# Plain blocks of a fused attention and two-layer MLP kernel: the second product two steps behind the first, s r + b in a buffer of its own, low halves of x on VectorE, attention's mean later

## The chip, the cores and the metric

The kernel runs on one core of a Trainium2 chip. A core has five engines that run side by side and meet at semaphores: TensorE (PE in the rows; its weight loads stand as PEld), VectorE (DVE), ScalarE (ACT), GpSimd (POOL) and SyncE (SP), whose queue issues every DMA here. Matrix products land in eight PSUM banks of 128 x 512 fp32 numbers, everything else is in SBUF or in DRAM. The metric is device time in microseconds (us), median of several runs.

## What is computed

Attention without softmax, normed by row, then two MLPs, all in fp32:

```python
kv = np.einsum('bhsd,bhse->bhde', k, v)          # 8 batches, 8 heads, 576 tokens, 64 wide
out = np.einsum('bhsd,bhde->bhse', q, kv)
out = out / np.sqrt(np.mean(out * out, axis=-1, keepdims=True) + 1e-06) * g_norm
x = out.transpose(0, 2, 1, 3).reshape(4608, 512)
r = np.maximum(x @ w_in, 0.0)                    # first MLP, 512 -> 2048 -> 512
x = (s * (r * r) + b) @ w_out
h = x @ w2_in                                    # second MLP, same sizes
y = (h * (1.0 / (1.0 + np.exp(-1.702 * h)))) @ w2_out
```

The weights arrive as 64-bit numbers and are brought to fp32 on ScalarE and VectorE.

## The kernel before

**Tiling.** The 4608 tokens are nine blocks of 512; features lie on the partitions, so a block of x is four tiles of 128 x 512. To keep fp32 accuracy at TensorE's faster format, each operand is split into a high part (rounded) and a low part (the rest): `xh`, `xl` of x, `gh`, `gl` of the activation, and two halves of each weight tile `w`. A product is then three matmuls: high by high, high by low, low by high.

**Stages.** The first MLP does blocks 0, 1, 2 plainly (`plain`) and the other six in pairs, with the first product by Strassen's seven products (`first_products`) and the second plainly (`second_plain`). The second MLP does four pairs with Strassen in both products and its last block plainly. Attention for block j is computed some time before block j is needed, in four units p (`attention`): `att_product` (o_ps), `att_square` (sq and, from block 2 on, its high part sh), `att_low` (sl), `att_mean` (ms, a product with a matrix of averages), `att_root` (three ScalarE steps), `att_newton` (three VectorE steps, after which the banks of o_ps and ms are free) and `att_split` (xh and xl, or a store to DRAM for blocks from 3 on). The K'V products of the later batches (`kv_product`, a tile kvs each) run between the steps of blocks 0 and 1.

**A plain block.** Sixteen steps f. `mlp_h` makes the first product of a step (twelve matmuls into a bank h), `mlp_act` relu and square into r, `mlp_g` the operand s r + b: gh from r on ScalarE (L447), then on VectorE r itself becomes s r + b in place (L448), then gl = r - gh (L451). `mlp_o` makes the second product of the step (twelve matmuls into four banks o that are summed over all steps); in the order of the program it stands one step behind the first product.

**Weights.** In block 0 both weights of each step are made from raw words: `w_low` (two ScalarE instructions, ca and cu), `w_words` (L144, L145, L150, L151 on VectorE), `w_hi` (L161, ScalarE) and `w_lo` (L166, VectorE). There are thirty such weights after the first two.

**What sets the order.** A table. Each piece of work is entered with a slot, a number (`at`); at the end the entries are sorted and written out, and each engine takes its own instructions in that order. A step of a plain block is two slots: the first product at 2f, activation and second product of the step before at 2f + 1. `kv_work` enters K'V loads and products, `attend` the units of attention with a list of seven gaps (product, square, low, mean, root, Newton, split) from the unit's first slot. `Slots` hands out PSUM banks and SBUF tiles, the one free longest first.

Of the kernel before, what the change touches and what calls it, by code (L numbers as in the profile page):

```python
# [7 lines left out]
F32 = mybir.dt.float32  # L8
# [3 lines left out]
ALU = mybir.AluOpType  # L12
# [5 lines left out]
NP = H // 2  # L18
NF = DFF // P
# [17 lines left out]
NBIG, NMID = 42, 22  # L37
NPLAIN = 3
LEAD = 4
G1_ACT = (0, 0, 0, 1.5, 0.2, 1.6, 1.6)  # L40
OPS = ("A11", "S2", "S3", "S1", "A12", "A22", "S4", "A21")
PRODUCTS = (("A11", "B11"), ("S2", "T2"), ("S3", "T3"), ("S1", "T1"), ("A12", "B21"), ("A22", "T4"), ("S4", "B22"))
# [18 lines left out]
def kernel(ctx: ExitStack, tc: tile.TileContext, qT, kv_h, kvt, cst,  # L61
# [7 lines left out]
    pe, act, dve, pool = nc.tensor, nc.scalar, nc.vector, nc.gpsimd  # L69
# [9 lines left out]
    def new(slots, shape, dtype, name):  # L79
        t, n = slots.take(shape, dtype, name)  # L80
        where[id(t)] = (slots, n, t)
        return t

    def drop(*tiles):
        for t in tiles:
            slots, n, _ = where.pop(id(t))
            slots.give(n)

    def new4(dtype, name):
        return new(big, [P, 2, T], dtype, name)  # L90

    def new2(dtype, name):
        return new(mid, [P, T], dtype, name)
# [8 lines left out]
    s_col, b_col = cst_sb[:, 1:2], cst_sb[:, 2:3]  # L102
# [267 lines left out]
    def att_split(j, p):  # L370
        x = att.pop((j, p))
        if j >= NPLAIN:
            nc.sync.dma_start(out=xd[0][j][p], in_=x)
            drop(x)
            done.add((0, j, p))
            return
        if p == 0:
            xT[0, j] = []
        if p % 2 == 0:
            xT[0, j].append((new4(F32R, "xh"), new4(F32R, "xl")))  # L380
        xh, xl = xT[0, j][p // 2]
        if j:
            act.activation(xh[:, p % 2, :], x, AF.Copy)
        else:
            dve.tensor_copy(out=xh[:, p % 2, :], in_=x)  # L385
        pool.tensor_sub(out=xl[:, p % 2, :], in0=x, in1=xh[:, p % 2, :].bitcast(F32))  # L386
        drop(x)
        done.add((0, j, p))

# [53 lines left out]
    def mlp_g(m, j, f):  # L443
        r = G[m, j, f]
        gh, gl = G[m, j, f] = new2(F32R, "gh"), new2(F32R, "gl")
        if m == 0:
            act.activation(gh, r, AF.Identity, scale=s_col, bias=b_col)  # L447
            dve.tensor_scalar(out=r, in0=r, scalar1=s_col, scalar2=b_col, op0=ALU.mult, op1=ALU.add)  # L448
        else:
            act.activation(gh, r, AF.Copy)  # L450
        dve.tensor_sub(out=gl, in0=r, in1=gh.bitcast(F32))  # L451
        drop(r)
# [218 lines left out]
    def at(slot, fn, *a):  # L671
        events.append((slot, len(events), fn, a))

    def weight(load, slot, gap, conv_at, *unit):
        at(load, w_load, *unit)
        for i, fn in zip(conv_at, (w_low, w_words, w_hi, w_lo)):
            at(slot + gap * i, fn, *unit)

    def kv_work(load, slot, b, p):
        at(load, kv_load, b, p)  # L680
        at(slot, kv_product, b, p)
        if b:
            at(slot + 2, kv_store, b, p)

    def attention(slots, j, p):
        for slot, fn in zip(slots, (att_product, att_square, att_low, att_mean, att_root, att_newton, att_split)):
            at(slot, fn, j, p)

    def plain(m, j, base, last):
        base -= 0.005  # L690
        for f in range(NF):
            at(base + 2 * f, mlp_h, m, j, f)
            at(base + 2 * f + 1, mlp_act, m, j, f)
            if f:
                at(base + 2 * f + 1, mlp_o, m, j, f - 1)
                if last:
                    at(base + 2 * f + 1, wo_done, m, f - 1)
            at(base + 2 * f + 1.01, mlp_g, m, j, f)
        end = base + 2 * NF + 1
        at(end - 0.01, mlp_o, m, j, NF - 1)  # L700
        if last:
            at(end - 0.01, wo_done, m, NF - 1)
        at(end + 0.02, mlp_store, m, j)

    def first_products(m, base, shift):
        for i in range(NF // 2):
            for k in range(len(PRODUCTS)):
                slot = base + 3.5 * i + 0.5 * k + (shift if i or k > 1 else 0)
                at(slot, g1_product, m, i, k)
                at(slot + 0.52, g1_sum, m, i, k)  # L710
                at(slot + 0.72 + G1_ACT[k], g1_act, m, i, k)
                if k % 2 == 0:
                    at(slot - LEAD, op_load, m, i, k // 2)
            if i % 2 and m == 0:
                for n, (q, fn) in enumerate((("22", AF.Relu), ("21", AF.Relu), ("22", AF.Square), ("21", AF.Square),
                                             ("12", AF.Relu), ("11", AF.Square), ("12", AF.Square))):
                    at(slot + 1.4 + 0.45 * n, r_act, q, i // 2, fn)
            elif i % 2:
                at(slot + 3.1, t_sums, i // 2)
        return base + 28 + shift  # L720

    def second_plain(j, base):
        for f in range(NF):
            at(base + 2 * f - LEAD, wo_load, 0, f)
            for n in range(2):
                slot = base + 2 * f + n
                at(slot, mlp_o, 0, j + n, f)
                if f % 4 < 2:
                    at(slot - 3.3, g2_scale, *quarter(f, n)[:2])
                at(slot - 2.5, g2_hi, 0, j + n, f, n)  # L730
                at(slot - 2.0, g2_lo, 0, j + n, f, n)
                if n:
                    at(slot, wo_done, 0, f)
        at(base + 31.1, mlp_store, 0, j)
        at(base + 32.1, mlp_store, 0, j + 1)
        return base + 32

    def second_products(j, base):
        for k in range(len(PRODUCTS)):
            for n in range(4):  # L740
                slot = base + 4 * k + n
                at(slot, g2_product, k, n)
                at(slot - LEAD, go_load, k, n)
                at(slot - 3.2, go_sum, k, n)
                at(slot - 2.4, go_hi, k, n)
                at(slot - 1.7, go_lo, k, n)
            for d in range(2):
                at(slot + 0.6 + 0.5 * d, g2_sum, j, k, d)
                if k > 2:
                    at(slot + 2.6, g2_store, j, k, d)  # L750
        return base + 28
# [55 lines left out]
    for p in range(NP):  # L807
        kv_work(-99 + p, START[p][0], 0, p)
        at(-99 + p, q_load, 0, p)
        o, m, n, x = START[p][1:]  # L810
# [2 lines left out]
    weight(-89, -48.5, 4, CONV[0], 0, 1, 0)  # L813


    for n, (f, w) in enumerate([(f - w, w) for f in range(1, NF + 1) for w in range(2) if f - w < NF][1:]):
        weight(n - 5, n - 1, 1, CONV[1], 0, f, w)


    for n in range(NP * (B - 1)):  # L820
        kv_work(2 * n - 8.9, 2 * n - 5, 1 + n // NP, n % NP)


    for j in range(NPLAIN):
        plain(0, j, 32 * j, j == NPLAIN - 1)
    base = 32 * NPLAIN
    firsts, seconds = {}, {}
    for j in range(NPLAIN, NB, 2):
        firsts[0, j] = base
        seconds[0, j] = first_products(0, base, j == NPLAIN)  # L830
        base = second_plain(j, seconds[0, j])
    for j in range(0, NB - 1, 2):
        firsts[1, j] = base
        seconds[1, j] = first_products(1, base, 0)
        base = second_products(j, seconds[1, j])
    plain(1, NB - 1, base, True)


    def attend(units, first, step, gaps):
        for u, (j, p) in enumerate(units):  # L840
            slot = first + step * u
            if p == 0 and j < B:
                at(slot - 2.2, kvbd_load, j)
            at(slot - 4, q_load, j, p)
            attention([slot + i for i in gaps], j, p)

    def units(*blocks):
        return [(j, p) for j in blocks for p in range(NP)]

    attend(units(1), 7, 6, (0, 0, 0, 2, 2, 4, 6))  # L850
    attend(units(2, 3), 34, 3.7, (0, 0.7, 1.3, 2, 2.5, 3.6, 6))
    attend(units(4), 65, 3, (0, 0.7, 1.3, 1.7, 2.2, 2.9, 4.5))
    for j in range(NPLAIN, NB - 2, 2):
        attend(units(j + 2, j + 3), firsts[0, j] + 0.4, 3.1, (0, 0.7, 1.3, 1.8, 2.3, 3.2, 5.5))


    x_operands(0, NPLAIN, 32 * NPLAIN - 14, 1.25)
# [11 lines left out]
    for k in range(2):  # L869
        slot = seconds[1, NB - 3] + 10 + 4 * k  # L870
# [10 lines left out]
    for i in range(NF // 2):  # L881
        slot = 50 + 5.4 * i
# [10 lines left out]
    slot = 32 * NPLAIN + 4  # L893
# [16 lines left out]

    for f in range(NF):
        at(base + 2 * f - LEAD, wi_load, 1, f)
        at(base + 2 * f + 2 - LEAD, wo_load, 1, f)

    events.sort(key=lambda e: e[:2])
    with tc.manual_schedule():
# [40 lines left out]
```

## Time and profile before

| | |
|---|---|
| median of 3 runs | 1606.41 us (1605.46 to 1606.84) |
| the profiled execution | 1604.21 us, of which the span from first to last instruction is 1602.4 us |
| TensorE busy | 1568.8 us, 98% of the span |
| VectorE busy | 1114.2 us, 70% |
| ScalarE busy | 846.3 us, 53% |
| GpSimd busy | 18.9 us, 1% |
| DMA | 385.36 MB, mean 240 GB/s |
| granted TensorE clock, mean | 0.996 of full |

The shares are means over stages that differ. Block 0 runs from about 28 to 167 us, block 1 to about 283, block 2 to about 383, then come the Strassen pairs, and the last plain block from about 1511 us on. In a row of the timeline the columns are start, duration, engine, line, operation, out<-in, shapes, count, and in brackets the engine's idle time just before and what ended it. Instructions of one engine overlap a little, so what one costs its engine is the distance to the next one's start.

### The profile page before, as it was taken

What the parts mean: (1) busy time and instruction counts of PE and PEld (TensorE: products, weight loads), DVE (VectorE), ACT (ScalarE), POOL (GpSimd) and SP (SyncE); (2) the same over time, 40 slices, a digit from 0 to 9 for tenths busy, and PEclk for the clock granted to TensorE, in tenths of its full rate; (3) what the DMA queues carried; (4) which work ended last, traced back from release to release, by engine and by line L of the source; (5) the groups of instructions that cost most, each with busy time, mean ns of one, the idle gap of its engine ahead of it and who ended that gap; (6) DMA issues with size and microseconds to landing.
All of it is one profiled execution on the core that took longest, in us unless ns stands there. A gap on an engine that the chain in (4) does not pass through costs nothing.

```text
span 1602.4 us, 19757 instructions
## 1 busy us (share of the span) xinstructions
PE 1568.8 (98%) x6932; PEld 1280.1 (80%) x6932; DVE 1114.2 (70%) x1621; ACT 846.3 (53%) x1261; POOL 18.9 (1%) x22
## 2 busy tenths in 40 slices
PE   7989999999999999999999999999999999999999
PEld 5766787778878887888888888888888888888887
DVE  6888346666888578784674378867986796688422
ACT  5767456655789468972694225512542353244222
POOL 1000000000000000000000000000000000000000
PEclk9999999999999999999999999999999999999999
DMA  7953646557978698976982585885688578736780
GB/s 239 308 183 103 207 150 206 205 195 246 326 282 294 220 383 286 323 252 262 342 307 80 203 302 200 285 301 212 238 270 302 187 276 274 270 120 220 240 293 27
DMA packets 172418, 385.36 MB, mean 240 GB/s; under 512 B 25120, under 2 KB 57888, under 8 KB 172320
## 3 DMA queue, kind: packets, MB, share of 16 engines
q1 hardware_dynamic: 172320, 384.11, 68.6%
q8 instruction: 55, 0.90, 0.2%
q14 instruction: 43, 0.35, 0.1%
HBM read 292.95 MB, written 91.10 MB: 240 GB/s over the span
## 4 chain that ended last, share of the span: by engine, by line
PE 60%; DVE 0%; issue 0%
PE o L632 19%; PE o L461 14%; PE d L504 7%; PE a L504 7%; PE b L504 3%; PE f L504 3%; PE c L504 3%; PE h L424 3%; DVE st L472 0%; DVE r L530 0%; DVE sl L342 0%; PE ms L350 0%; DVE op L229 0%
## 5 line engine op out<-in xcount | busy, mean ns | idle before, releaser
L461 PE MATMUL o<-gh,w 128*128 128x512 f32 x1280 | 407.5, 391 | 0.3
L461 PEld LDWEIGHTS o<-gh,w 128*128 128x128 f32 x1280 | 240.4, 188 | 51.8 <-ACT gh L447 2.0
L632 PE MATMUL o<-gh,wl 128*128 128x512 f32 x896 | 276.7, 389 | 0.0
L461 PE MATMUL o<-gl,w 128*128 128x512 f32 x640 | 251.0, 392 | 10.5 <-DVE gl L451 10.3
L632 PEld LDWEIGHTS o<-gh,wl 128*128 128x128 f32 x896 | 168.2, 188 | 34.9
L424 PE MATMUL h<-xh,w 128*128 128x512 f32 x512 | 176.7, 406 | 0.2 <-DVE xh L385 0.2
L632 PE MATMUL o<-gl,wl 128*128 128x512 f32 x448 | 174.5, 389 | 0.0
L504 PE MATMUL a<-xh,wl 128*128 128x512 f32 x448 | 157.5, 392 | 0.7 <-ACT c L520 0.7
L504 PE MATMUL d<-xh,wl 128*128 128x512 f32 x448 | 157.2, 392 | 0.3 <-DVE r L530 0.3
L461 PEld LDWEIGHTS o<-gl,w 128*128 128x128 f32 x640 | 120.2, 188 | 40.6 <-DVE gl L451 15.5
L424 PEld LDWEIGHTS h<-xh,w 128*128 128x128 f32 x512 | 97.3, 190 | 24.2 <-issue 1.0
L520 ACT ACTIVATE c<-a 128x512 f32<-128x512 f32 x56 | 33.3, 595 | 156.6 <-PE a L504 156.6
L424 PE MATMUL h<-xl,w 128*128 128x512 f32 x256 | 101.3, 396 | 1.9 <-POOL xl L386 1.9
L504 PEld LDWEIGHTS a<-xh,wl 128*128 128x128 f32 x448 | 84.1, 188 | 18.9 <-ACT c L520 1.1
L504 PEld LDWEIGHTS d<-xh,wl 128*128 128x128 f32 x448 | 84.1, 188 | 18.3 <-DVE r L530 0.8
L632 PEld LDWEIGHTS o<-gl,wl 128*128 128x128 f32 x448 | 84.1, 188 | 17.4
L575 DVE TENSOR_TENSOR gl<-r,gh 128x512 fp32r<-128x512 f32 x96 | 65.1, 688 | 38.8 <-ACT gh L570 36.8
L606 ACT ACTIVATE gh<-t 128x1024 fp32r<-128x1024 f32 x48 | 51.0, 1062 | 72.4 <-DVE t L597 62.3
L504 PE MATMUL a<-xl,wl 128*128 128x512 f32 x224 | 87.3, 390 | 0.0
L504 PE MATMUL d<-xl,wl 128*128 128x512 f32 x224 | 87.3, 390 | 0.0
L559 ACT ACTIVATE r<-r 128x1024 f32<-128x1024 f32 x84 | 84.8, 1047 | 0.0
L611 DVE TENSOR_TENSOR gl<-r,gh 128x1024 fp32r<-128x1024 f32 x64 | 77.2, 1219 | 7.2 <-ACT gh L606 7.2
(110 smaller groups left out, 2701.0 us busy)
## 6 DMA issues: line engine op xcount, KB each, us to landing
wl<-wsd SPq DMA_DIRECT2D x168, 512.0 KB, 7.0
wl<-wo2S SPq DMA_DIRECT2D x64, 512.0 KB, 5.7
wsd<-op SPq DMA_DIRECT2D x96, 256.0 KB, 3.8
w<-wod SPq DMA_DIRECT2D x48, 512.0 KB, 6.3
wl<-wo2A SPq DMA_DIRECT2D x48, 512.0 KB, 4.8
raw<-in_w_in SPq DMA_DIRECT2D x32, 512.0 KB, 7.1
kv_in<-in_kv SPq DMA_DIRECT2D x32, 512.0 KB, 4.9
raw<-in_w_out SPq DMA_DIRECT2D x32, 512.0 KB, 6.3
```

Source lines behind the costliest of these rows:

```text
L424: pe.matmul(h, lhsT=a, rhs=b, start=(n == 0), stop=(n == 3 * NP - 1))
L461: pe.matmul(acc[m, j][c], lhsT=a, rhs=x, start=(f == 0 and n == 0), stop=(f == NF - 1 and n == 2))
L504: pe.matmul(o, lhsT=a, rhs=b, start=(first and n == 0), stop=(n == 5), skip_group_check=not first)
L520: act.activation(st["c1"], st[0], AF.Copy)
L559: act.activation(R[q, n], R[q, n], fn)
L575: dve.tensor_sub(out=gl, in0=R[q, i][:, half, :], in1=gh.bitcast(F32))
L606: act.activation(hi, src, AF.Copy)
L611: dve.tensor_sub(out=lo, in0=src, in1=hi.bitcast(F32))
L632: pe.matmul(so[k, d], lhsT=a, rhs=b, start=(first and n == 0 and i == 0 and e == 0), stop=(n == 3 and i == 1 and e == 2), skip_group_check ...
```

## The change

`LAG = 2`: in a plain block the second product of step f stands at slot 2f + 4.99, two steps behind the first and not one; the store of the block's sums moves with it, and so do, by the same constant, the loads and the making of second weights, and the two places where the last plain block of the first MLP runs into the Strassen part (`first_products`' shift). `mlp_g` of the first MLP writes s r + b into a new tile g. The subtraction xl = x - xh goes from GpSimd to VectorE. K'V loads and products from the fourth on stand two slots later (product) and 2.4 slots later (load). Attention's units of block 1 start at 9.2, every 5 slots (before: 7, every 6), those of the first Strassen pair at 5.4 every 2.9 slots behind its start (before: 0.4 and 3.1), and the gaps change: mean, root and Newton step of blocks 2 to 4 stand about 0.5 to 0.8 slots later behind their product.

```diff
@@ att_split
-        pool.tensor_sub(out=xl[:, p % 2, :], in0=x, in1=xh[:, p % 2, :].bitcast(F32))
+        dve.tensor_sub(out=xl[:, p % 2, :], in0=x, in1=xh[:, p % 2, :].bitcast(F32))
@@ mlp_g
             act.activation(gh, r, AF.Identity, scale=s_col, bias=b_col)
-            dve.tensor_scalar(out=r, in0=r, scalar1=s_col, scalar2=b_col, op0=ALU.mult, op1=ALU.add)
+            g = new2(F32, "g")
+            dve.tensor_scalar(out=g, in0=r, scalar1=s_col, scalar2=b_col, op0=ALU.mult, op1=ALU.add)
+            drop(r)
+            r = g
@@ plain
-            if f:
-                at(base + 2 * f + 1, mlp_o, m, j, f - 1)
...
+            slot = base + 2 * f + 2 * LAG + 0.995
+            at(slot, mlp_o, m, j, f)
...
+        at(slot + 0.03, mlp_store, m, j)
@@ first_products
-                slot = base + 3.5 * i + 0.5 * k + (shift if i or k > 1 else 0)
+                slot = base + 3.5 * i + 0.5 * k + min(shift, (7 * i + k) // 2)
@@ weights, K'V and attention's slots
-    for n, (f, w) in enumerate([(f - w, w) for f in range(1, NF + 1) for w in range(2) if f - w < NF][1:]):
+    for n, (f, w) in enumerate([(f - LAG * w, w) for f in range(1, NF + LAG) for w in range(2) if 0 <= f - LAG * w < NF][1:]):
-        kv_work(2 * n - 8.9, 2 * n - 5, 1 + n // NP, n % NP)
+        kv_work(2 * n - (8.9 if n < 3 else 6.5), 2 * n - (5 if n < 3 else 3), 1 + n // NP, n % NP)
-    attend(units(1), 7, 6, (0, 0, 0, 2, 2, 4, 6))
-    attend(units(2, 3), 34, 3.7, (0, 0.7, 1.3, 2, 2.5, 3.6, 6))
-    attend(units(4), 65, 3, (0, 0.7, 1.3, 1.7, 2.2, 2.9, 4.5))
+    attend(units(1), 9.2, 5, (0, 0.2, 0.2, 1.8, 2, 3.6, 5.5))
+    attend(units(2, 3), 34, 3.7, (0, 0.7, 1.3, 2.6, 3.0, 4.0, 6))
+    attend(units(4), 65, 3.2, (0, 0.7, 1.3, 2.3, 2.7, 3.7, 5))
...
-        attend(units(j + 2, j + 3), firsts[0, j] + 0.4, 3.1, (0, 0.7, 1.3, 1.8, 2.3, 3.2, 5.5))
+        first, step = (5.4, 2.9) if j == NPLAIN else (0.4, 3.1)
+        attend(units(j + 2, j + 3), firsts[0, j] + first, step, (0, 0.7, 1.3, 1.8, 2.3, 3.2, 5.5))
@@ second weights of the last plain block
-        at(base + 2 * f + 2 - LEAD, wo_load, 1, f)
+        at(base + 2 * f + 2 * LAG - LEAD, wo_load, 1, f)
```

The order on ScalarE in block 0, in the step in which the first unit of block 1's attention takes its root (y), before (r is relu and square, w and ca, cu belong to weights):

```order
L436 ACTIVATE r<-h 128x512
L437 ACTIVATE r<-r 128x512
L161 ACTIVATE w<-ca 128x512
L297 ACTIVATE kvs<-kv 64x64
L357 ACTIVATE y<-ms,eps 128x512
L358 ACTIVATE y<-y 128x512
L359 ACTIVATE y_765<-y 128x512
L447 ACTIVATE gh<-r,cst_sb 128x512
L137 ACTIVATE ca<-raw 128x512
```

The same step after (lines are those of the changed file):

```order
L437 ACTIVATE r<-h 128x512
L438 ACTIVATE r<-r 128x512
L162 ACTIVATE w<-ca 128x512
L298 ACTIVATE kvs<-kv 64x64
L448 ACTIVATE gh<-r,cst_sb 128x512
L358 ACTIVATE y<-ms,eps 128x512
L359 ACTIVATE y<-y 128x512
L360 ACTIVATE y_826<-y 128x512
L138 ACTIVATE ca<-raw 128x512
```

The three steps of the root have moved from ahead of gh to behind it.

The order on VectorE in block 0, where that unit's Newton steps stand, before:

```order
L300 COPY kvs<-kv 64x64
L364 SCALAR_TENSOR_TENSOR y_765<-ms,y_765 128x512
L365 SCALAR_TENSOR_TENSOR y<-y_765,y 128x512
L366 SCALAR_TENSOR_TENSOR y_765<-o_ps,g_col,y 128x512
L448 TENSOR_SCALAR r<-r,cst_sb 128x512
L451 TENSOR_TENSOR gl<-r,gh 128x512
L166 TENSOR_TENSOR w<-ca,w 128x512
L144 TENSOR_SCALAR cu<-cu 128x512
```

And after:

```order
L301 COPY kvs<-kv 64x64
L450 TENSOR_SCALAR g<-r,cst_sb 128x512
L455 TENSOR_TENSOR gl<-g,gh 128x512
L167 TENSOR_TENSOR w<-ca,w 128x512
L145 TENSOR_SCALAR cu<-cu 128x512
L146 TENSOR_SCALAR cu<-cu 128x512
L151 SCALAR_TENSOR_TENSOR cu<-raw,cu 128x512
L152 ISA ca<-cu,ca 128x1024
L167 TENSOR_TENSOR w<-ca,w 128x512
L365 SCALAR_TENSOR_TENSOR y_826<-ms,y_826 128x512
L366 SCALAR_TENSOR_TENSOR y<-y_826,y 128x512
L367 SCALAR_TENSOR_TENSOR y_826<-o_ps,g_col,y 128x512
```

The Newton steps have moved from ahead of the step's gl to behind it and behind a weight, and the scaling writes g.

## Rows read from the trace of the kernel before

**Rows 1.** Busy time by stretch: us, busy of each engine, PEclk, DMA share, GB/s

```profile
33.00:164.00 131.00, 116.76 (x528) 89.94 (x529) 114.61 (x208) 92.28 (x167) 5.44 (x4) 0.97 0.64 203
166.00:283.00 117.00, 114.44 (x531) 92.04 (x530) 58.04 (x95) 64.78 (x111) 6.50 (x5) 1.00 0.55 185
283.00:383.00 100.00, 94.87 (x411) 77.74 (x410) 65.65 (x105) 58.43 (x89) 0.00 (x0) 0.98 0.57 196
383.00:480.00 97.00, 95.03 (x415) 76.41 (x414) 77.22 (x129) 74.61 (x113) 0.00 (x0) 1.00 0.88 307
460.00:510.00 50.00, 48.97 (x215) 39.93 (x214) 40.69 (x69) 49.84 (x70) 0.00 (x0) 1.00 0.75 265
600.00:800.00 200.00, 199.75 (x873) 163.65 (x873) 146.88 (x246) 140.42 (x204) 0.00 (x0) 1.00 0.83 294
328.20:331.50 3.30, 3.30 (x10) 2.56 (x9) 1.74 (x3) 1.32 (x3) 0.00 (x0) 0.50 0.90 286
```

**Rows 2.** TensorE's waits up to 480 us: us in total, times, longest

```profile
PE o L461 <- DVE gl L451: 10.3, 8, 2.1
PE ms L350 <- DVE sl L342: 8.6, 7, 2.9
PE kv L287 <- DMA kv_in<-in_kv: 2.9, 1, 2.9
...
PE a L504 <- ACT c L520: 0.7, 1, 0.7
```

**Rows 3.** Timeline of VectorE, one step of block 0 without attention

```profile
48.48 0.23 DVE L300 COPY kvs<-kv 64x64 f32<-64x64 f32 x1
...
49.93 0.68 DVE L166 TENSOR_TENSOR w<-ca,w 128x512 fp32r<-128x512 f32 x1
50.53 0.42 DVE L144 TENSOR_SCALAR cu<-cu 128x512 f32<-128x512 f32 x1
...
52.17 0.69 DVE L151 CUSTOM_DVE_ANT_0 ca<-cu,ca 128x1024 uint16<-128x1024 uint16 x1
52.79 0.68 DVE L166 TENSOR_TENSOR w<-ca,w 128x512 fp32r<-128x512 f32 x1
```

**Rows 4.** Timeline, VectorE's last weight and TensorE's way into block 1

```profile
163.22 0.68 DVE L166 TENSOR_TENSOR w<-ca,w 128x512 fp32r<-128x512 f32 x1
...
166.01 1.05 PE L287 MATMUL kv<-kv_in 128*128 128x128 f32 x8
...
167.40 0.50 PE L424 MATMUL h<-xh,w 128*128 128x512 f32 x1
```

**Rows 5.** Timeline of VectorE, Newton steps of two units of block 1's attention

```profile
107.83 0.69 DVE L364 SCALAR_TENSOR_TENSOR y<-ms,y 128x512 f32<-128x512 f32 x1
...
109.95 0.54 DVE L448 TENSOR_SCALAR r<-r,cst_sb 128x512 f32<-128x512 f32 x1
...
134.53 0.69 DVE L364 SCALAR_TENSOR_TENSOR y<-ms,y 128x512 f32<-128x512 f32 x1
```

**Rows 6.** VectorE's waits from 33 to 165 us, all that the view lists

```profile
DVE r L448 <- ACT gh L447: 10.7, 7, 2.1
DVE kvs L300 <- ACT kvs L297: 1.0, 1, 1.0
```

**Rows 7.** Timeline, VectorE and GpSimd where xl is made

```profile
32.58 1.20 DVE L144 TENSOR_SCALAR cu<-cu 128x512 f32<-128x512 f32 x1
...
89.14 1.29 POOL L386 TENSOR_TENSOR xl<-y,xh 128x512 fp32r<-128x512 f32 x1 [55.64 <-DVE cu L150]
89.15 1.82 DVE L151 CUSTOM_DVE_ANT_0 ca<-cu,ca 128x1024 uint16<-128x1024 uint16 x1
```

**Rows 8.** Timeline in block 2, VectorE's scaling and TensorE's mean

```profile
302.87 0.54 DVE L448 TENSOR_SCALAR r<-r,cst_sb 128x512 f32<-128x512 f32 x1 [3.05 <-ACT gh L447]
...
305.40 0.49 PE L350 MATMUL ms<-sl,ones 128*128 128x512 f32 x1 [2.86 <-DVE sl L342]
```

More of the change, by code (lines that the diff above doesn't have):

```diff
@@ L39 @@
 LEAD = 4
+LAG = 2
 G1_ACT = (0, 0, 0, 1.5, 0.2, 1.6, 1.6)
@@ L693, in plain @@
             at(base + 2 * f + 1, mlp_act, m, j, f)
-            if f:
-                at(base + 2 * f + 1, mlp_o, m, j, f - 1)
-                if last:
-                    at(base + 2 * f + 1, wo_done, m, f - 1)
             at(base + 2 * f + 1.01, mlp_g, m, j, f)
[L699 to L703, printed above, removed]
+            slot = base + 2 * f + 2 * LAG + 0.995
+            at(slot, mlp_o, m, j, f)
+            if last:
+                at(slot, wo_done, m, f)
+        at(slot + 0.03, mlp_store, m, j)
     def first_products(m, base, shift):
@@ L829 @@
         firsts[0, j] = base
-        seconds[0, j] = first_products(0, base, j == NPLAIN)
+        seconds[0, j] = first_products(0, base, LAG if j == NPLAIN else 0)
         base = second_plain(j, seconds[0, j])
```

## The prediction

> **What bounds the kernel now.** I read busy time by stretch, then TensorE's waits, then VectorE's timeline. In a late stretch with hardly a wait TensorE does 873 matmuls in 200 us [rows 1], 0.229 us each, so the twelve matmuls of one first or second product of a plain step take 2.75 us. What it loses lies before 480 us: in 33 to 164 us it is idle for 131.0 - 116.8 = 14.2 us, in 166 to 283 for 2.6, in 283 to 383 for 5.1, in 383 to 480 for 2.0 [rows 1]. Behind these stand two waits above all: the second product waits for the low half gl of its input (10.3 us), and attention's mean waits for sl (8.6 us); the Strassen part adds 0.7 for a copy c [rows 2]. Nothing after 480 us can give more than a few tenths.
>
> In 33 to 164 us another engine is nearly as full: VectorE, 114.6 of 131.0 us [rows 1]. It makes the weights there. One weight (five instructions) takes 52.79 - 49.93 = 2.86 us, and the copy kvs, the scaling and gl together 49.93 - 48.48 = 1.45 us [rows 3], so a step with two weights costs it 2 x 2.86 + 1.45 = 7.17 us, while TensorE needs 2 x 2.75 + 1.39 = 6.89 (1.39 for a K'V product is 167.40 - 166.01 [rows 4]). A unit of attention adds 109.95 - 107.83 = 2.12 us on VectorE [rows 5]. So block 0 is VectorE's stage: taking away a wait of TensorE there is worth only what VectorE is then also spared.
>
> **Block 0, part by part.** VectorE's idle time in 33 to 165 us is 10.7 us before the scaling, waiting for gh on ScalarE, and 1.0 us before kvs [rows 6], 11.7 in all. The scaling waits because it writes over r, which gh still reads. With a buffer g of its own it needs only the square. The gl behind it still needs gh, but ScalarE now makes gh right behind its K'V copy, ahead of the three steps of attention's root, which stood before it. So I let most of the 11.7 us go.
>
> The low half of x goes from GpSimd to VectorE. A GpSimd instruction lengthens the VectorE instruction beside it: 0.42 us became 1.20 at 32.58, 0.69 became 1.82 at 89.15, where xl began on GpSimd at 89.14 [rows 3, 7]; that is 0.8 and 1.1 us spared. VectorE pays for each xl about the 0.68 us of its nearest row, the weight's low half (two inputs, same shape) [rows 3]. Before the first product's weights it pays four of them, 2.7 us, and is spared some 1.7 us, so the stretch starts 1.0 us later (bounds -1 to 2.7). Inside the stretch three more cost 2.0 us, and 1.9 are spared.
> A rule that speaks against this edit is in the Trainium skill, Perfetto Trace Analysis, Optimizing Scalar/DVE Operations: work should leave a saturated VectorE, for ScalarE or even GpSimd; it adds that the port VectorE shares with GpSimd may undo the gain. By its first half the edit costs seven times 0.68 = 4.8 us; the rows above, with their 0.8 and 1.1 us, side with its second half.
>
> The last weight of block 0 ends at 163.22 + 0.68 = 163.90 us [rows 4]. Now: 163.9 + 1.0 - 11.7 - 1.9 + 2.0 - 0.3 (one K'V copy has moved out) = 153.0, 10.9 us earlier. TensorE can't run much ahead: from slot 12 to 28 most h products take a bank that relu or attention's Newton step gave back only a slot or so earlier, as the lists of free banks show. So block 1's first product, at 167.40 now [rows 4], also moves by about 10.9 us. But with the lag of two, one second product (2.75) and one K'V product (1.39) less has been done by then: 10.9 - 4.1 = 6.8 us gained. For gh that still comes late, and ScalarE's root, I keep 1.8 us: **5.0 us** gained. Bounds: 6.8, and if all 11.7 us stay, 163.9 + 1.0 - 1.9 + 2.0 - 0.3 = 164.7, 0.8 later, a loss of 0.8 + 4.1 = 4.9.
>
> What the lag needs is there. Weights of one kind come 3.5 slots before their use instead of 2.5. K'V loads move on SP behind two raw loads; the 2.9 us that TensorE waits for one at 37 us [rows 2] may stay, but VectorE sets the pace there, so I count nothing (bounds 0 and 2.9, either side).
>
> **Blocks 1 and 2: the mean.** In 166 to 283 us TensorE's 2.6 idle us are three waits of a mean for sl, and in 283 to 383 the 5.1 us are two more [rows 1, 2]. One is seen at 305.40: sl stood on VectorE behind gl, and that behind a scaling that waited 3.05 us for gh; the mean then waited 2.86 us [rows 8]. After the other the granted clock was 0.50, 1.2 GHz of 2.4, for the 3.3 us from 328.2 to 331.5 [rows 1], which costs half of them, 1.6. The change puts the mean 0.6 slots later (a slot is 2.75 us and up here), and in block 2 two whole products now stand between a unit's product and its mean, 5.5 us; and the scaling ahead of sl no longer waits for gh, though gl does. I keep 0.2 of 2.6 and 0.4 of 5.1 + 1.6: **2.4 and 6.3 us** gained; at worst I'd keep half. The last unit of block 4's attention, made during block 2, now stores x only 0.4 slots before SP loads it, so SP may stand until that store has landed; its operands are needed 14 slots later, so this costs nothing.
>
> **First products (383 to 480 us).** Attention starts five slots later, at a slightly closer step, and its last root now falls behind the last copy c instead of before it. ScalarE is full here, 49.84 of 50 us in 460 to 510 [rows 1], and TensorE waits 0.7 us for c [rows 2]. The root leaves c's path and stands before a gh instead; no second product of that part waits for gl now [rows 2], all such waits lie before 166 us. I count **0.5 us** gained, between all of the 2.0 idle us and as much again lost. Behind 480 us, and in the last plain block, nothing waits: zero.
>
> **Sum.** 5.0 + 2.4 + 6.3 + 0.5 = 14.2 us from the profiled execution's 1604.2 (span 1602.4): 1590.0. The median of the three runs stands 2.2 above the profiled one, so the median after should be **1592.2**. Best case of all terms: 6.8 + 2.6 + 6.7 + 2.0 = 18.1, 1588.3.
>
> **Rivals.** A: VectorE's waits merely change their name (gl waits for gh, where r waited). Then block 0 loses 4.9 instead of gaining 5.0, and only the mean's gain is left: 1602.1. For it: gl still needs gh, and ScalarE's copy kvs ahead of gh waits for TensorE. Against it: gh waits were longest where the root stood before it [rows 6], and it doesn't any more.
> B, **slower**: the bank loop in block 0. A unit of attention holds two banks until its Newton step; from the freed bank it is one h, one o_ps, a second product, a K'V product, another h and the mean, then root and Newton, before the next unit gives its bank back. Units began 134.53 - 107.83 = 26.7 us apart for three steps [rows 5]; now they come every two and a half. If they stayed 26.7 us apart, three intervals would carry 7.5 steps and not 9; the 1.5 steps left over cost 1.5 x 7.17 = 10.8 us more, with the 4.1 us 14.9 lost, 9.2 gained elsewhere: 1612.1. It decides once the loop is longer than VectorE's own 2.5 x 7.17 + 2.12 + 0.68 = 20.7 us per unit. By rows it is about 3 x 2.75 + 1.39 + 2 for o_ps and mean, 2 for the root (three steps, taken as long as the Newton step's three), 2.12: 15.8. The Trainium skill (Perfetto Trace Analysis, Optimization Strategy) reads equal gaps that repeat on a saturated engine as a possible lack of buffers for the next tile; the waits for gl, up to 2.1 us, that come back with every unit look like it, but the profile puts all eight down to gl [rows 2].
> C: VectorE isn't the bound, and all 14.2 idle us of block 0 go: 9.2 better than forecast, 1583. Against it are the sums above.
>
> **Chances.** Forecast (block 0 gains 1 to 7, 1587 to 1597) 0.66; A, in part or whole (1597 to 1603) 0.18; no change 0.05; B 0.06; C 0.05. The range 1587 to 1600 leaves out B, C, no change and the end of A. This kernel can't be told from unchanged within 0.2% (3.2 us): faster 0.88, same 0.06, slower 0.06.
>
> **What will show it.** The last weight's low half at 152 to 156 us, VectorE busy for over 92% from 33 us to there; second products wait under 2 us for gl; waits of means for sl under 1.5 us; no granted clock of 0.5 near 330 us; if ScalarE's c copy at the last first products comes later than now, the fourth term is wrong. I am wrong if VectorE still stands 10 us for gh, or if h waits for banks.

## The result and the profile after

The kernel after takes 1591.54 us (median of four runs, 1590.96 to 1591.88), the kernel before in the same series 1605.93 (1604.97 to 1606.84): a ratio of 0.991, 95% interval 0.9893 to 0.9927. The forecast was 1592.2 in a range of 1587 to 1600. The profiled execution took 1591.87 us with a span of 1590.1; by the sum it should have been 1590.0. So the total came out 1.9 us longer than the sum, and the median close to the forecast because the kernel before's profiled execution, 1604.21, had been one of its quicker ones: the medians differ by 14.4 us, the two profiled executions by 12.3.

The total is right, several of the terms are not. TensorE's passage through four places tells the shares. These are rows of its timeline after: the first h of block 1, the first Strassen product, the first second product of the Strassen part, and the same one of the next pair (start, duration, engine, line, operation).

```profile
161.08 0.50 PE L425 MATMUL h<-xh,w 128*128 128x512 f32 x1
...
370.38 0.39 PE L508 MATMUL a<-xh,wl 128*128 128x512 f32 x1
...
463.57 0.39 PE L465 MATMUL o<-gh,w 128*128 128x512 f32 x1
...
639.54 0.39 PE L465 MATMUL o<-gh,w 128*128 128x512 f32 x1
```

Three of the same rows before (the first of the four is in [rows 4], 167.40):

```profile
383.42 0.39 PE L504 MATMUL a<-xh,wl 128*128 128x512 f32 x1
...
476.50 0.40 PE L461 MATMUL o<-gh,w 128*128 128x512 f32 x1
...
651.60 0.39 PE L461 MATMUL o<-gh,w 128*128 128x512 f32 x1
```

Work that the lag and the later K'V products push over a border is set against this: 4.1 us into block 1 (a second product, 2.72, and a K'V product, 1.39), and one second product more, 2.72, over the border at 370.38.

| stage | before to after, us | moved work | gained | forecast |
|---|---|---|---|---|
| up to block 1 | 167.40 to 161.08 | 4.1 left for later | 2.2 | 5.0 |
| blocks 1 and 2 | 216.0 to 209.3 | 4.1 in, 2.7 out | 8.1 | 2.4 + 6.3 |
| first Strassen products | 93.1 to 93.2 | 2.7 more | 2.6 | 0.5 |
| next pair | 175.1 to 176.0 | none | -0.9 | 0 |
| rest of the span | 950.8 to 950.6 | none | 0.2 | 0 |

Together 12.3 us (2.2 + 8.1 + 2.6 - 0.9 + 0.2 is 12.2 with these rounded terms), the difference of the two spans.

The table compares one execution of each kernel. Two kernels of the experiments below do the same work in the same order as the kernel before up to block 1: the one with only attention's mean later, and the one with only attention's slots in the first Strassen part. Their first h of block 1:

```profile
170.10 0.50 PE L424 MATMUL h<-xh,w 128*128 128x512 f32 x1
...
168.43 0.50 PE L424 MATMUL h<-xh,w 128*128 128x512 f32 x1
```

In the kernel before it comes at 167.40. So block 0's gain is between 2.2 and 4.9 us, by which execution is taken for before; part of why they differ is told in the last section. Blocks 1 and 2, 216.0 us before, take 217.4 in the second of them. From the first Strassen product on the traces agree better: in the kernel before and in three kernels of the experiments that change nothing there (attention's mean later, buffer and xl, order alone) the first Strassen products take 93.07 to 93.12 us.

Busy time by stretch after, the borders of [rows 1] moved with the stages (us, then busy time of TensorE, its weight loads, VectorE, ScalarE and GpSimd, granted clock, DMA share, GB/s):

```profile
33.00:155.00 122.00, 109.68 (x495) 87.24 (x495) 113.03 (x208) 87.94 (x161) 0.00 (x0) 0.94 0.65 204
155.00:272.00 117.00, 115.78 (x546) 94.53 (x545) 58.35 (x104) 62.98 (x110) 0.00 (x0) 1.00 0.61 198
272.00:372.00 100.00, 98.86 (x436) 81.31 (x435) 69.13 (x112) 62.65 (x96) 0.00 (x0) 1.00 0.62 210
372.00:469.00 97.00, 96.73 (x426) 78.72 (x425) 75.30 (x126) 74.69 (x113) 0.00 (x0) 1.00 0.86 307
325.00:335.00 10.00, 10.00 (x45) 8.27 (x45) 6.02 (x9) 5.34 (x8) 0.00 (x0) 1.00 0.78 256
```

Idle time in blocks 1 and 2 is 1.2 and 1.1 us (2.6 and 5.1 before), 0.3 in the first products (2.0), and the half clock near 330 us is gone. Block 0 still loses 12.3 us of 122, at a lower mean clock than before. TensorE's waits after, up to 480 us, the largest three and the one for sl:

```profile
PE h L425 <- DVE y L367: 7.8, 2, 4.2
PE kv L288 <- DMA kv_in<-in_kv: 5.4, 2, 4.3
PE h L425 <- DVE xh L386: 2.3, 1, 2.3
...
PE ms L351 <- DVE sl L343: 1.6, 3, 0.7
```

Against [rows 2]: no second product waits for gl (10.3 us before), and means wait 1.6 us for sl (8.6). In their place h waits for attention's Newton step, twice: the bank that it writes into is the one that this step gives back. And VectorE's waits from 33 to 158 us, all that are listed:

```profile
DVE xl L387 <- ACT xh L384: 1.6, 2, 1.0
DVE cu L145 <- ACT cu L139: 1.5, 2, 0.8
DVE kvs L301 <- ACT kvs L298: 0.2, 1, 0.2
```

3.3 us, where [rows 6] has 11.7. The last weight of block 0 after (before: 163.22 [rows 4]):

```profile
157.67 0.69 DVE L167 TENSOR_TENSOR w<-ca,w 128x512 fp32r<-128x512 f32 x1
```

### The profile page after: what moved, and what is told of

Its sections match the earlier page's. It is cut to its first block, busy times and chain, and to the rows that moved or that the text cites. A ratio compares the mean times of both kernels' runs of the same rounds, so it can differ in the third digit from the quotient of the medians.

```text
span 1590.1 us, 19815 instructions
## 1 busy us (share of the span) xinstructions
PE 1563.4 (98%) x6932; PEld 1280.9 (81%) x6932; DVE 1114.2 (70%) x1633; ACT 844.7 (53%) x1261; POOL 1.7 (0%) x10
## 4 chain that ended last, share of the span: by engine, by line
PE 69%; ACT 1%; DVE 1%; issue 0%; DMA 0%; SPq 0%; DVEq 0%; ACTq 0%
PE o L465 19%; PE o L636 19%; PE d L508 8%; PE a L508 8%; PE f L508 4%; PE b L508 4%; PE c L508 4%; PE h L425 3%; ACT r L563 1%; PE o_ps L323 0%; DMA wl<-wsd 0%; PE ms L351 0%; ACT y L359 0%; ACT y L358 0%; DVE r L534 0%
## 5 line engine op out<-in xcount | busy, mean ns | idle before, releaser
L508 PE MATMUL a<-xh,wl 128*128 128x512 f32 x448 | 157.6, 392 | 0.0
```

Source lines behind the costliest of these rows:

```text
L508: pe.matmul(o, lhsT=a, rhs=b, start=(first and n == 0), stop=(n == 5), skip_group_check=not first)
```

## Experiments

Median times below are of four to ten runs; the kernel before ran beside each group (medians 1605.74, 1605.70 and 1605.60 us), and intervals are of the ratio to it. Differences from the kernel after are from its 1591.54 us, measured beside a median of 1605.93. Stage times are of one profiled execution each.

### The low half of x back on GpSimd

```diff
-        dve.tensor_sub(out=xl[:, p % 2, :], in0=x, in1=xh[:, p % 2, :].bitcast(F32))
+        pool.tensor_sub(out=xl[:, p % 2, :], in0=x, in1=xh[:, p % 2, :].bitcast(F32))
```

> The kernel after with one edit undone: the low half xl of x is made on GpSimd again. My theory (VectorE sets the pace of block 0, and a GpSimd instruction lengthens the VectorE instruction beside it by about as much as VectorE itself would need): 1590.4 to 1592, within 1.5 us of the kernel after (1591.5), with some 16 GpSimd instructions that each make one VectorE instruction about 0.8 to 1.1 us longer. Rival, the rule that work should leave a saturated VectorE: about 4.8 us faster, 1586.7. Second rival, that the edit is a real part of the gain: 1594 or more.

1593.30 us (0.9907 to 0.9937), 1.8 slower than after. VectorE by operation from 33 us to the last weight, here (count | busy us, mean ns | idle before, us):

```profile
L151 DVE SCALAR_TENSOR_TENSOR cu<-raw,cu 128x512 uint32<-128x512 uint32 x30 | 22.7, 756 | 1.0
L167 DVE TENSOR_TENSOR w<-ca,w 128x512 fp32r<-128x512 f32 x30 | 21.6, 721 | 0.0
L145 DVE TENSOR_SCALAR cu<-cu 128x512 f32<-128x512 f32 x30 | 13.4, 447 | 4.0 <-ACT cu L139 3.9
L455 DVE TENSOR_TENSOR gl<-g,gh 128x512 fp32r<-128x512 f32 x15 | 11.4, 762 | 1.6
```

and in the kernel after:

```profile
L151 DVE SCALAR_TENSOR_TENSOR cu<-raw,cu 128x512 uint32<-128x512 uint32 x30 | 20.8, 693 | 1.0
L167 DVE TENSOR_TENSOR w<-ca,w 128x512 fp32r<-128x512 f32 x30 | 20.5, 685 | 0.0
L145 DVE TENSOR_SCALAR cu<-cu 128x512 f32<-128x512 f32 x30 | 12.6, 421 | 1.6 <-ACT cu L139 1.5
L455 DVE TENSOR_TENSOR gl<-g,gh 128x512 fp32r<-128x512 f32 x15 | 10.4, 693 | 1.5
```

Four GpSimd instructions in the stretch lengthen VectorE's by 1.9 + 1.1 + 0.8 + 1.0 = 4.8 us, 1.2 each, against 0.69 for an xl on VectorE itself. The edit is a real part of the gain, as the second rival has it, though the time lies above my theory's range and short of that rival's 1594; the bill of 0.8 to 1.1 us each was too low. Block 1 begins at 163.07 us, 2.0 later than after, and the stages behind it are as long as there. The Trainium skill (Perfetto Trace Analysis, Optimizing Scalar/DVE Operations) lets work leave a saturated VectorE even for GpSimd, and remarks that a port shared by the two may undo the gain: the runs side with the remark.

### The buffer g taken away

```diff
-            g = new2(F32, "g")
-            dve.tensor_scalar(out=g, in0=r, scalar1=s_col, scalar2=b_col, op0=ALU.mult, op1=ALU.add)
-            drop(r)
-            r = g
+            dve.tensor_scalar(out=r, in0=r, scalar1=s_col, scalar2=b_col, op0=ALU.mult, op1=ALU.add)
```

> The kernel after with one edit undone: VectorE again writes s r + b over r, without the buffer g. My theory: the scaling then has to wait for gh on ScalarE as before, and since VectorE sets the pace of block 0, most of that comes back as time: VectorE waits 5 to 10 us more on r in block 0, the last weight of block 0 ends 3 to 8 us later than 158, total 1594 to 1599. Rival (the lag of two steps does the work, and gh, now ahead of the root on ScalarE, is ready in time anyway): under 1 us slower, 1591 to 1592.5.

1593.20 us (0.9906 to 0.9939), 1.7 slower. But not in block 0: VectorE's wait for gh there, with r written in place, is

```profile
DVE r L449 <- ACT gh L448: 0.5, 1, 0.5
```

and the last weight starts at 157.6 us as in the kernel after (157.7). The time lies between the ranges of theory and rival. TensorE's additional idle time, 1.3 us, is in blocks 1 and 2, where its means wait 0.5 us more for sl and 0.7 more for a bank that Newton's step gives back; by the start of the first h and of the first Strassen product (160.66 and 371.97 us) the two blocks take 2.0 us longer than after:

```profile
155.00:272.00 117.00, 115.40 (x544) 94.10 (x543) 57.08 (x102) 62.85 (x110) 0.00 (x0) 1.00 0.61 197
272.00:372.00 100.00, 97.96 (x429) 79.95 (x428) 67.71 (x111) 62.55 (x95) 0.00 (x0) 1.00 0.59 201
```

The theory that g frees VectorE in block 0 falls; the next two kernels ask what does.

### Buffer and xl alone, order alone, in the kernel before

The first adds g and the xl on VectorE to the kernel before (the two edits above, the other way round). The second changes one number in it:

```diff
-    attend(units(1), 7, 6, (0, 0, 0, 2, 2, 4, 6))
+    attend(units(1), 7.2, 6, (0, 0, 0, 2, 2, 4, 6))
```

> The kernel before with two edits of the change alone: the buffer g for s r + b, and xl on VectorE. Attention's root still stands ahead of gh on ScalarE, and the lag is one. Theory formed on the runs so far (the order on ScalarE decides, not the buffer): VectorE's waits only change their name, 8 to 11 us on gl for gh in place of r, and the time is 1603 to 1606. Rival, the step of the prediction (the scaling then needs only the square, and gl finds gh ready): VectorE waits under 4 us and the time is 1596 to 1600.

> The kernel before with one number changed: the units of block 1's attention start at 7.2 instead of 7, every 6 slots as before. That puts mean and root 0.2 slots later, so that on ScalarE gh stands ahead of the three steps of the root; no buffer g, no lag, xl on GpSimd. Theory (the order on ScalarE is what makes VectorE wait): VectorE's wait for gh falls from 10.7 us to under 3, the last weight of block 0 ends 5 to 8 us earlier than 163.9, and the time is 1597.5 to 1601. Rival (the buffer and the lag are needed): over 1604.

Buffer and xl alone: 1603.75 us (0.9974 to 0.9993), 2.0 faster than before. Time and waits are as the theory expected. VectorE's wait changed its name, as rival A of the prediction says:

```profile
DVE gl L454 <- ACT gh L447: 9.6, 7, 2.0
DVE kvs L300 <- ACT kvs L297: 2.6, 4, 1.0
```

In this trace block 1 begins at 169.77, within the 167.4 to 170.1 us of the old block 0, and blocks 1 and 2 take 213.3 us instead of 216.0: what these two edits gain stands there.

Order alone: 1601.94 us (0.9966 to 0.9986), 3.8 faster. gh now stands ahead of the root on ScalarE:

```profile
DVE cu L144 <- ACT cu L138: 4.7, 4, 1.4
DVE kvs L300 <- ACT kvs L297: 2.3, 4, 0.9
DVE r L448 <- ACT gh L447: 2.2, 5, 0.6
```

So the order on ScalarE is what removes the wait for gh, 10.7 to 2.2 us. Yet other waits come up, and there are 9.2 us of them in all; the VectorE instructions beside GpSimd's xl are longer too, and the last weight starts at 163.12, as before (163.22). Of my expectation only the wait came: the last weight did not move, and the time lies between the two ranges. But the profiled execution took 1603.98 us, 2.0 above its median, and its span, 1602.2, is that of the kernel before (1602.4). The 3.8 us are not in this trace, so it does not show where they are gained. In it block 1 begins at 165.55, 1.9 us earlier, and blocks 1 and 2 take 1.6 us longer. Which of the other edits of block 0 (K'V products two slots later, attention's step of five) brings the rest I did not try alone.

### The lag back to one step

```diff
-LAG = 2
+LAG = 1
```

> The kernel after with LAG = 1: the second product one step behind the first again, everything else as in the kernel after. Theory (VectorE sets the pace of block 0, so the lag changes TensorE's waits and not the time): second products wait for gl again, up to 3 us in all, and the time is within 2 us of the kernel after, 1590 to 1593.5. Rival (the lag is what gained): second products wait 6 us or more for gl and the time is 1596 to 1600.

1591.95 us (0.9898 to 0.9928), 0.4 above the kernel after, whose range it overlaps. Its TensorE at the same places:

```profile
161.51 0.50 PE L425 MATMUL h<-xh,w 128*128 128x512 f32 x1
...
369.75 0.39 PE L508 MATMUL a<-xh,wl 128*128 128x512 f32 x1
...
463.20 0.39 PE L465 MATMUL o<-gh,w 128*128 128x512 f32 x1
```

At block 1 it is 0.43 us later with a whole second product more behind it: 2.3 us ahead of the kernel after. It gains 4.5 us there (167.40 - 161.51 - 1.39), near the 5.0 of the forecast. Its waits: for gl 3.3 us and gh 2.0 (more than the 3 that I expected), but for Newton's bank only 3.2 (7.8 after) and for a K'V load 0.2 (5.4):

```profile
PE o L465 <- DVE gl L455: 3.3, 2, 2.0
PE h L425 <- DVE y L367: 3.2, 2, 1.6
...
PE o L465 <- ACT gh L448: 2.0, 1, 2.0
...
PE kv L288 <- DMA kv_in<-in_kv: 0.2, 1, 0.2
```

It gives this back in the first Strassen products, 93.45 us with one second product where the kernel after needs 93.19 with two: 3.0 us. In the other direction the lag of two costs 1.1 us in blocks 1 and 2 (209.30 for 208.24) and 0.9 in the next pair (175.97 for 175.08). So the lag is worth nothing in sum; it moves a gain from one stage to another.

### Attention's mean back, and later in the kernel before

The first kernel is the kernel after with these two lines undone, the second the kernel before with them alone:

```diff
-    attend(units(2, 3), 34, 3.7, (0, 0.7, 1.3, 2, 2.5, 3.6, 6))
-    attend(units(4), 65, 3, (0, 0.7, 1.3, 1.7, 2.2, 2.9, 4.5))
+    attend(units(2, 3), 34, 3.7, (0, 0.7, 1.3, 2.6, 3.0, 4.0, 6))
+    attend(units(4), 65, 3.2, (0, 0.7, 1.3, 2.3, 2.7, 3.7, 5))
```

> The kernel after with attention's gaps and step of blocks 2, 3 and 4 as they were (mean, root and Newton step 0.6 slots closer to the product). Theory: means wait for sl again in blocks 1 and 2, 4 to 9 us slower, 1595.5 to 1600.5, with a granted clock of half in one place. Rival: the buffer g has already freed sl on VectorE, since the scaling ahead of it no longer waits, so that the gaps matter little: 1591.5 to 1593.

> The kernel before with the gaps and the step of attention for blocks 2, 3 and 4 of the change alone, nothing else. By the prediction's terms 8.7 us faster, 1597; by the run that put the gaps back (4.9 us) 4 to 6 us faster, 1599.5 to 1601.5, since without the buffer g a scaling that waits for gh still holds up sl. If less than 2 us, the mean waits for sl here for another reason than its slot.

Undone: 1596.48 us (0.9928 to 0.9958), 4.9 slower, and the wait is back, though no half clock with it:

```profile
PE ms L351 <- DVE sl L343: 6.2, 5, 2.3
```

Alone: 1600.49 us (0.9955 to 0.9981), 5.1 faster. Both runs give the gaps 5 us. They are the largest of the edits that were tried alone. By stage, blocks 1 and 2 take 4.7 us longer with the gaps undone (214.0 for 209.3) and 6.0 less with them alone (210.1 for 216.0).

### Attention's slots in the first Strassen part, alone

```diff
-        attend(units(j + 2, j + 3), firsts[0, j] + 0.4, 3.1, (0, 0.7, 1.3, 1.8, 2.3, 3.2, 5.5))
+        first, step = (5.4, 2.9) if j == NPLAIN else (0.4, 3.1)
+        attend(units(j + 2, j + 3), firsts[0, j] + first, step, (0, 0.7, 1.3, 1.8, 2.3, 3.2, 5.5))
```

> The kernel before with attention's slots in the first Strassen part alone moved (first 5.4, step 2.9 in place of 0.4 and 3.1). By the prediction 0.5 us faster; by the stage times of the kernel after 2.6 us faster, 1603; by the run with lag one, where that stage was as long as before with the new slots, 0: other waits (sl, a copy of K'V) take the place of the wait for c: 1605.2 to 1606.2.

1605.62 us (0.9991 to 1.001): nothing that the total shows, whose interval is 1.5 us to either side. In the trace the stage takes 92.52 us (385.80 to 478.32) where the kernels with the old slots take 93.07 to 93.12: the 0.5 us of the forecast. The wait for c is gone, and the one wait of TensorE left in that part is 1.4 us (before: 0.9 for sl, 0.7 for c, 0.3 for r):

```profile
PE ms L350 <- DVE sl L342: 1.4, 2, 1.1
```

The 2.6 us of this stage in the kernel after come only with the lag of two: in the kernel with the lag back to one the same new slots left waits of 1.4 us for sl and 0.6 for a K'V copy in it. A lag of two with the old slots was not run.

### VectorE given more and less to do in block 0

The first kernel computes gl twice in each step of block 0, the second copies both halves of kvs on ScalarE:

```diff
-        dve.tensor_sub(out=gl, in0=r, in1=gh.bitcast(F32))
+        for _ in range(2 if m == 0 and j == 0 else 1):
+            dve.tensor_sub(out=gl, in0=r, in1=gh.bitcast(F32))
```

```diff
             act.activation(lo, kv[0:D, 0:D], AF.Copy)
+            act.activation(hi, kv[D:P, D:P], AF.Copy)
         else:
             dve.tensor_copy(out=lo, in_=kv[0:D, 0:D])
-        dve.tensor_copy(out=hi, in_=kv[D:P, D:P])
+            dve.tensor_copy(out=hi, in_=kv[D:P, D:P])
```

> The kernel after with one VectorE instruction more in each of block 0's sixteen steps: gl is computed twice, 0.69 us each, 10.4 us over the fifteen steps up to the last weight. Theory (VectorE sets the pace, its remaining waits of 3.3 us may take up a part): 6 to 10.4 us slower, 1597.5 to 1602. Rival (a loop through the PSUM banks sets it, VectorE has room): under 3 us slower.

> The kernel after with one more edit: both halves of kvs are copied on ScalarE, so VectorE is spared 29 copies of 64 x 64, 17 of them (0.23 us and 0.03 of gap each, 4.4 us) in block 0. Theory (VectorE sets the pace of block 0): the last weight of block 0 is 2 to 4.4 us earlier and the time 1587 to 1589.5. Rival (TensorE's bank waits or ScalarE set it by now): 1591 to 1593.

More: 1599.89 us (0.9945 to 0.9974), 8.4 slower for 10.4 us of work; the last weight starts at 167.18, 9.5 later. Less: 1590.04 us (0.9883 to 0.9913), 1.5 faster for 4.4 us; the last weight starts at 154.18, 3.5 earlier, block 1's first h at 157.91, 3.2 earlier. VectorE now waits 5.8 us instead of 3.3:

```profile
DVE cu L145 <- ACT cu L139: 2.5, 4, 1.2
DVE xl L388 <- ACT xh L385: 2.0, 2, 1.0
DVE gl L456 <- ACT gh L449: 0.8, 1, 0.8
DVE ca L152 <- DVE cu L151: 0.5, 1, 0.5
```

VectorE sets the pace of block 0: more work shows almost fully, and in that kernel VectorE waits only 2.0 us in all up to 166 us, so it is not held up by the banks (TensorE's wait for Newton's bank grows from 7.8 to 12.0). Less work shows too, 3.2 of 4.4 us, as far as block 1. The total keeps half of that, and so lies between my two ranges: 0.6 us are lost in the first Strassen products (93.74 for 93.19), and 0.8 behind TensorE's last matmul, which starts 4.9 us before the end of the span instead of 4.2. Why was not traced; only the two kernels with the copies on ScalarE have this longer end.

### The bank that h waits for

Newton's step 0.25 slots later, in the kernel after, and the same together with the copies on ScalarE:

```diff
-    attend(units(1), 9.2, 5, (0, 0.2, 0.2, 1.8, 2, 3.6, 5.5))
+    attend(units(1), 9.2, 5, (0, 0.2, 0.2, 1.8, 2, 3.85, 5.5))
```

> The kernel after with one number changed: Newton's step of block 1's attention 3.85 slots behind its product in place of 3.6. For the first and third unit it then stands behind a K'V product and a relu in the program, so that the next h takes the bank of an older h and not the one that Newton gives back. Both theories expect the waits of h for Newton, 7.8 us in two places, to go, and with them the two stretches of half clock near 83 and 131 us. Theory (VectorE sets the pace of block 0): the time hardly moves, 1590.5 to 1592. Rival (the bank waits are the cause of the part of block 0's gain that did not come): 3 to 6 us faster, 1585.5 to 1588.5.

> The kernel after with both: kvs copied on ScalarE alone (1.5 us faster by itself) and Newton's step at 3.85. Theory (VectorE sets the pace, but with the copies gone TensorE's waits are nearly as long a chain): more than the sum of the two, 1586.5 to 1589. Rival (ScalarE now sets the pace: VectorE waited 5.8 us for it with the copies moved): 1589.5 to 1590.5.

Alone: 1591.32 us (0.9899 to 0.9929), within the spread of the kernel after. Both theories had expected the waits of 7.8 us to go. They moved, in part to the product o_ps, and 5.7 us stayed:

```profile
PE o_ps L323 <- DVE y L367: 2.9, 1, 2.9
PE h L425 <- DVE y L367: 2.8, 1, 2.8
```

The last weight starts at 154.85, 2.8 us earlier, and still block 1's first h comes at 161.37, no earlier than after: here it is TensorE that is late, for part of the way at half clock (0.58 from 154.4 to 157.6 us). So this kernel does not tell what the bank waits cost.

Together: **1587.38 us** (1585.67 to 1587.75; 0.9871 to 0.9901), 4.2 faster than after, and more than the two apart (1.5 + 0.2). Last weight and first h of block 1:

```profile
149.89 0.69 DVE L167 TENSOR_TENSOR w<-ca,w 128x512 fp32r<-128x512 f32 x1
...
155.19 0.50 PE L426 MATMUL h<-xh,w 128*128 128x512 f32 x1
```

5.9 us earlier than after. At 457.66 us, the first second product of the Strassen part, all 5.9 are still there; the span is 4.8 shorter, so 1.1 us are lost behind it, 0.8 of them behind TensorE's last matmul. It beats both kernels. What it shows: both engines limit block 0. Up to block 1's first h the two edits apart gain 3.2 us and lose 0.3, and together they gain 5.9. How much of this is TensorE's clock, which differs between these executions, is not shown.

## Why the total was right and the terms were not

**Block 0: 5.0 forecast, 2.2 measured, or up to 4.9 from the other executions of the same block.** The time of this term is not far off, then, but three steps of it failed.

- *Why VectorE waited.* "With a buffer g of its own it needs only the square" took the wrong cause. With the buffer alone gl waits 9.6 us for gh; without it, in the new order, r waits 0.5. The second reason that the prediction gave, gh ahead of the root on ScalarE, is the one that the order-alone kernel shows, and in its one trace, of a long execution, it does not bring the last weight forward by itself.
- *The size.* The last weight ends at 157.67 + 0.69 = 158.36 us and not at 153.0. Of the 5.4 us, 3.3 are waits that stayed under new names (cu and xl for ScalarE), 0.7 a fourth xl in the stretch where I had counted three, and 1.0 the gap ahead of gl (1.5 us in all after, 0.5 before); 0.4 are not traced. From the two other executions of the old block 0, with their last weights at 165.90 and 164.26, the last weight moved by 8.2 and 6.6 us and not by 5.6; the forecast was 10.9. The sign that the prediction named, the last weight at 152 to 156 us, did not come; VectorE's busy share of over 92% did (113.0 of 122 us).
- *The lag.* The prediction gave it no price but the moved work. It costs block 0 2.3 us, by the run with a lag of one (one execution of each): h waits for Newton's bank, which the text itself named as the sign of being wrong. It is the mechanism of rival B in small: two waits of about 4 us, where B had 14.9. And the wait for a K'V load, left at 2.9 us without a price, became 5.4, in two places; with a lag of one it is 0.2.

That TensorE's entry into block 1 follows VectorE's last weight held in these two kernels: 5.6 and 6.3 us earlier. It is no rule: with the order alone the entry came 1.9 us earlier and the last weight 0.1, and with Newton's step later the weight came 2.8 earlier and the entry not at all.

**Blocks 1 and 2: 8.7 forecast, 8.1 measured.** The waits for sl, the two products in between, and the lost half clock came as described (1.6 us of waits for sl stayed, where the forecast's sign was under 1.5). The runs split it: in the stage itself the gaps alone gain 6.0 us and their loss costs 4.7; the buffer g, with xl, gains 2.7 alone, and its loss costs 2.0. Its use is here and not in block 0. One execution of the same two blocks took 1.4 us longer than the kernel before's, so the split is no finer than that.

**First products: 0.5 forecast, 2.6 measured.** The term was right for what it priced: the new slots alone shorten the stage by 0.5 us. It left out the lag, whose shift of the whole Strassen part by one more slot was costed as nothing. With a lag of one the new slots leave the stage 0.4 us longer than before, with a lag of two it gains 2.6; 1.7 of these are waits of TensorE that went (idle 2.0 us before, 0.3 after), the rest was not traced.

**The next pair: 0 forecast, 0.9 lost.** This goes with the lag too: all six traced kernels with a lag of one take 175.1 us here, all eight with a lag of two 175.9 to 176.4. In the kernel after TensorE's weight loads for the products d wait 1.1 us for r on VectorE (L534), which they did not before. Why the lag makes r late stays open.

**xl.** Costed at 1.0 - 1.9 + 2.0, a loss of 1.1 us; it gains 1.8, as a GpSimd instruction costs VectorE 1.2 us and not 0.95, and as ScalarE's cu waits fall too.

**Sum**, between the two profiled executions. 2.8 us too much in block 0, 0.6 in the blocks behind it, 0.9 lost in the next pair of Strassen blocks, 2.1 too little in the first products: that is the 1.9 us by which the profiled execution missed 1590.0, within rounding. That the errors nearly cancel is luck: the terms do not bear out a forecast as near as the 0.7 us between the medians. The single edits in the kernel before give 5.1 + 3.8 + 2.0 + 0.0 = 10.9 of the 14.4 us; the rest comes only with the edits together, or with those of block 0 that were not tried alone.

## What to carry to other kernels

Where an instruction waits for another engine, ask what stands ahead of the producer in that engine's own order before giving the consumer a buffer: here one number in the table did more than the buffer. Where two engines are about equally full, price an edit against both, and try the edit for either one together with that for the other. A fixed order of free banks turns a change of a quarter of a slot into another bank, and so into another wait; after every shift of the table, look for new waits on buffers.

## What the runs showed of the hardware

A wait of TensorE can cost more than itself. The prediction had one such place, near 330 us [rows 1]; the kernel after has larger ones in block 0. These are the stretches around the wait that ended at 85.30 us in the kernel after (columns as above, the granted clock third from the end):

```profile
78.00:82.80 4.80, 3.10 (x18) 2.48 (x17) 4.56 (x9) 4.71 (x9) 0.00 (x0) 1.00 0.69 174
82.80:89.60 6.80, 4.30 (x10) 3.44 (x11) 6.45 (x12) 2.84 (x6) 0.00 (x0) 0.50 0.40 135
```

TensorE stood from 81.1 to 85.3; from 82.8 to 89.6 the granted clock was 0.50, 1.2 GHz of 2.4, so that the matmuls behind the wait ran at half speed; from 89.6 to 95 it was 1.00 again. In the fastest kernel, which has no such wait there, the same stretch reads 1.00 (it has two other stretches at half clock, near 73 and 107 us):

```profile
82.80:89.60 6.80, 6.80 (x34) 5.39 (x34) 6.52 (x12) 4.96 (x9) 0.00 (x0) 1.00 0.81 245
```

The wait alone does not decide it. The kernel before and the kernel with only attention's mean later have the same order of matmuls up to block 1, and in both TensorE waits 2.09 us for gl, until 84.19 us in the first and 83.87 in the second. The stretch behind it, first before, then with the mean later:

```profile
85.20:88.20 3.00, 3.00 (x18) 2.47 (x16) 2.90 (x6) 0.63 (x1) 0.00 (x0) 1.00 0.81 286
85.20:88.20 3.00, 3.00 (x10) 2.42 (x9) 2.86 (x7) 0.63 (x1) 0.00 (x0) 0.50 0.73 250
```

The second does 10 matmuls where the first does 18. The same happens near 113 us, behind the next of these waits (1.00 and 0.50 from 112.8 to 115.8 us). VectorE, 0.3 us ahead of the kernel before until the first of the two, is 0.8 us behind it after the first and 2.3 after the second. So the times of a stage in single executions differ by up to 2.7 us with nothing changed in it, and a difference of that size between two traces is not yet an effect of the edit.
